# An mLSTM, a soft mixture of experts and a squared-ReLU MLP on one core: the output weights' remainders, two clears and the last copy are moved

## The chip, the cores and the metric

The kernel runs on one core of a Trainium2 chip. The metric is the device time of one execution in microseconds (us), lower is better. A core has five engines that run their own instruction streams in order and wait for each other by semaphores: TensorE (PE in the rows, its weight loads PEld), VectorE (DVE), ScalarE (ACT), GpSimd (POOL) and SyncE (SP). Here all DMAs are issued by SyncE. Matmuls write to PSUM, and everything else lies in SBUF.

## The reference

Three steps over 4 sequences of 768 tokens, 3072 tokens of width 320 in all. `logits`, `d` and `c` are those of a soft mixture: 32 slots gather weighted sums of tokens, 8 experts turn them into outputs, and each token takes a weighted sum of the slots.

```python
# 1. mLSTM with a stabilised exponential gate, 8 heads of 40: y
# 2. soft mixture of experts
logits = x @ phi                                   # x: 3072 x 320, phi: 320 x 32
d = exp(logits - logits.max(0)); d /= d.sum(0) + 1e-9
slot_input = (d.T @ x).reshape(E, 4, D)            # E = 8
for e in range(E):
    slot_out[e] = np.maximum(slot_input[e] @ w1[e], 0.0) @ w2[e]
c = exp(logits - logits.max(1)); c /= c.sum(1) + 1e-9
x = c @ slot_out.reshape(32, D)
# 3. MLP
r = np.maximum(x @ w_in, 0.0)                      # w_in: 320 x 2048
return (r * r) @ w_out                             # w_out: 2048 x 320
```

## The kernel before

**Stages.** From 0 to some 151 us of the profiled span the mLSTM runs chunk by chunk, with the mixture's first three sequences filled in between. From there to some 183 us (the passage, below) the last sequence's logits, the token sums, the experts and the preparation of the MLP follow each other. From 183 us to the end the MLP loop runs: 96 steps, 6 groups of 512 tokens (`tg`) by 16 blocks of 128 hidden features (`f`). Each step has one matmul for a later step's hidden block (L1472) and twelve for the output (L1546): four blocks of 128 tokens, three products each, since both factors are split into a rounded part and a remainder (`hi` and `los`, `wohl["h"]` and `wohl["l"]`).

**The order of the work is written out by hand** (a manual schedule): each engine runs its instructions in the order in which the code issues them. Generators are pieces of work advanced by `next` and run out by `finish`. `cgo(n)` advances the building of the table `cst[n]` of mixing weights (L1122 and L1124 on VectorE, transposes L1130 on TensorE, copy L1135 on ScalarE). The passage's own path is: token sums (L1229), `combine`, `ffn_up(0)` and `ffn_up(1)` (the experts' first matmuls, L1221, by halves of the hidden features), `relu` (L1276), `ffn_tr` (transposes, then the copy L1333 into the block-padded `hT`), `ffn_down(0)` to `ffn_down(7)` (L1350, all eight into one PSUM bank), the copy `sos` (L1402), its transposes (L1407) with the copies into `soT` (L1410), and `gp_mm` (L1428), the first matmul of the MLP.

**The output weights.** `w_out` comes as 16 blocks of 128 rows, and is rounded and split in pairs of blocks, 640 columns each; `f` names a pair by its first block. Each pair takes `narrow`: two ScalarE instructions (L144, L148) into two scratch tiles, and two of VectorE (L152, L156) that put them together; then `wo_put`: a ScalarE cast (L1385) gives the rounded part, and a VectorE subtraction (L1386) the remainder. Pairs 0, 2 lie in `wo0`, 4 in `x3`, 6 in `xTw`; pairs 8, 10 come into `stage` by one load, `load_wo(stage, 8, 4)`, and 12, 14 into `par` by another (L905, 128 x 2560 words, 1.31 MB each). `stage` holds expert weights that `ffn_down(0)` reads, so its load is issued behind that. Before the change pairs 0 to 6 are narrowed in the passage, all with the one scratch pair `par_t`, and put in it (6 excepted); pairs 8 to 14 are made in the MLP loop at the steps that `X8` and `WO` name.

**What else the change touches.** `xf` (an old token buffer, `x` in the rows) is cleared by VectorE for the slots' padded inputs ahead of the token sums (L1199); `hT` (in `ring`) is cleared by GpSimd (L1291); `repm`, a 0/1 matrix, is built by VectorE (L1279, L1284); `call_last` finishes the last mixing weights; the loop's output copies (L1555) are ScalarE's.

Of the kernel before, what the change touches and what calls it, by code (L numbers as in the profile page):

```python
# [8 lines left out]
F32 = mybir.dt.float32  # L9
# [19 lines left out]
AHEAD = 3  # L29
UP = ((2, 3), (4,))  # L30
MODE = "fffaaaaaaaaaaaaa"
W8 = 0
GM, GA = (0, 1, 4, 6), (1, 3)
W6, X8 = 3, (2, 4)
WO = (5, 7, 10)
LAST = {3: "PADNgGG", 2: "gGGA", 1: ""}
START = "~36 1f 1i 1m 1h 1p 1b 1aG 1B 1r 1u 1A 1v D0 2f 1l T0 T1 1q M0 2i E0 W0 K0 D0 M1 E1 ~6 2m D0 2p 2b 2aG K1 W2 P0 2h D0 2B 2r 2u P1 M2 2v E2 2A 2l K2 ~7 | 3f 3i D1 ~6 | D1 2q 3m 3h 3p | D1 3b 3aG 3B 3r | 3u D1 3A 3l 3v | D2 3q | D2 | D2 | D2 X |"
REBIAS = 2.0**-112
# [7 lines left out]
def kernel(  # L46
# [1149 lines left out]
        nc.vector.tensor_copy(craw(B1) if m else en[:, m].rearrange("p u s -> p (u s)"), t[:, 0:192])  # L1196

    nc.vector.tensor_reduce(out=se4[96:128], in_=t2[96:128, 0:B1], axis=AX.X, op=ALU.add)
    nc.vector.memset(xf[:, FF : FF + 80 * NE], 0.0)  # L1199
    tr_el(0)  # L1200
    finish(fd)
    warm(WD[4], dumt)
# [76 lines left out]
    nc.vector.tensor_scalar(  # L1279
        out=repm, in0=ident[:, 0:1].to_broadcast([128, 64 + 4 * 128]), scalar1=0.0, scalar2=None, op0=ALU.mult  # L1280
    )
    for n in range(4):
        for r in range(2):
# [8 lines left out]
    for n in range(6):
        ld_w2(ring_half(2 * (n % 3) + n // 3), *w2o[10 + n])
    cgo(1, 1)
    t = bank("m")
    nc.tensor.matmul(t[:, 0:1], lhsT=selJ.rearrange("p j i -> p (j i)"), rhs=rt[0:32], start=True, stop=True)
    nc.vector.tensor_copy(rt128, t[:, 0:1])
    relu(0)
    finish(wo_narrow(2, *par_t))
    tr_el(1)  # L1300
    lg = call[:, NC * (B1 - 1) : NC * B, :]
    cm = mp.tile([128, 12], F32, tag="cm", name="cm")
    nc.vector.tensor_reduce(out=cm, in_=lg, axis=AX.X, op=ALU.max)
    cc = el_.rearrange("p m t -> p (m t)")[:, 0:384].rearrange("p (n s) -> p n s", s=32)
    nc.vector.tensor_tensor(out=cc, in0=lg, in1=cm.unsqueeze(2).to_broadcast([128, 12, 32]), op=ALU.subtract)
# [87 lines left out]

    ffn_down(1)
    load_wo(par[1][:, 0:SLOT], 12, 4)
    wo_put(0)
    ffn_down(2)
    ffn_down(3)
    wo_put(2)
    for f in range(4, 8):  # L1400
        ffn_down(f)
    nc.scalar.copy(sos, so[:, 0:DM])  # L1402
    cgo(3, 3, 5)
    dumf = bank("o")
# [8 lines left out]
                .rearrange("p (j s) -> p j s", j=NP)[:, :, 0:8],  # L1413
            )
    cgo(4, 5, 4)
    wo_put(4)
    ws8 = wo_split(8)
    for _ in range(W8):
        next(ws8)
    gc = [slice(0, 128), slice(128, 512)]  # L1420
    gps = [bank("mb"), bank("m")]

# [91 lines left out]
        g_rep(n, gc[1], trep[:, 0:384])  # L1514
        (nc.scalar.copy if n in GA else nc.vector.tensor_copy)(gst[n + 1], trep[:, 0:384])

    def put6():
        yield
        wo_put(6)

    wos = {W6: [(put6(), 9)], X8[0]: [(ws8, 4 - W8)]}
    wos.setdefault(X8[1], []).append((ws8, 9))
    for k, b in enumerate(WO):
        wg = wo_split(10 + 2 * k)
        for d, n in ((0, 4), (1, 2), (2, 9)):
            wos.setdefault(b + d, []).append((wg, n))

    acc = None
    for i, (tg, f) in enumerate(steps):
        if len(UP) <= i < len(steps) - AHEAD:  # L1530
            up(*steps[i + AHEAD])
        for wg, n in wos.get(i, ()):
            for _ in range(n):
                next(wg, None)
        if f == 0:
            acc = [bbank("acc") for _ in range(4)]
        hi, lo = gh.pop((tg, f)), gl.pop((tg, f))
        ua = [(u, a) for u in range(4) for a in range(3)]
        if i == 0:
            ua.sort(key=lambda x: (x[0] // 2, x[1]))  # L1540
        for n, (u, a) in enumerate(ua):
            if i == 0 and n == 3:
                gp_mm(1, 2)
                gp_hl(1)
            l_, r_ = ((hi, "h"), (hi, "l"), (lo, "h"))[a]
            nc.tensor.matmul(  # L1546
                acc[u][:, 0:DM],
                lhsT=l_[:, 128 * u : 128 * u + 128],
                rhs=wohl[r_, f // 8][:, f % 8, :],
                start=(f == 0 and a == 0),  # L1550
                stop=(f == NF - 1 and a == 2),
            )
# [95 lines left out]
```

## Time and profile before

| | |
|---|---|
| median of 3 runs | 383.35 us (383.09 to 383.78) |
| the profiled execution | 383.42 us, of which the span from first to last instruction is 381.70 |
| granted TensorE clock | 1.00 |
| busy over the span | TensorE 373.2 us (98%), VectorE 265.1 (69%), ScalarE 257.8 (68%), GpSimd 102.3 (27%) |

Times in the rows are microseconds from the start of the span. TensorE's "busy" takes the modelled ends of its matmuls, so a busy stretch can hide a loss of some tenths; where it stood still it shows as an idle time in brackets behind a row, with the instruction that ended it. An engine's idle time matters only if TensorE, or the last DMA, waits for it.

### The profile page before, as it was taken

The page shows a single profiled execution, that of the slowest core. Times are in us where ns is not written, and L with a number is a line of the kernel's source. Part 1 is how long each engine was busy: PE and PEld are TensorE (multiplying, and loading weights), DVE is VectorE, ACT ScalarE, POOL GpSimd, SP SyncE. Part 2 cuts the span into 40 slices and gives each one's busy share as a digit, 9 for nine tenths or more (in the row PEclk, how much of TensorE's full clock was granted, in tenths as well). Part 3 has the DMA queues.
Part 4 walks back from the last instruction along what each step waited for, and adds up shares of the span by engine and source line. Part 5 has one row for each costly group of instructions (what it writes and reads, how often), then busy time and mean ns, then how long its engine had stood idle before and what let it go on. Part 6 is the DMA issues. An engine that isn't in the chain of part 4 may idle for free.

```text
span 381.7 us, 9179 instructions
## 1 busy us (share of the span) xinstructions
PE 373.2 (98%) x3435; PEld 333.0 (87%) x3435; DVE 265.1 (69%) x596; ACT 257.8 (68%) x592; POOL 102.3 (27%) x207
## 2 busy tenths in 40 slices
PE   8999999999999999999999999999999999999996
PEld 6889998889889886445799899999999999999996
DVE  7878888979898478667798955555555555555551
ACT  7798766668656855365797966576675667667662
POOL 5665976766677465200000000000000000000000
PEclk9999999999999999999999999999999999999999
DMA  6796897899959998895000020020020001002001
GB/s 180 229 345 209 286 318 221 261 328 341 327 172 374 316 388 300 290 371 244 3 0 0 2 69 3 0 70 1 2 69 2 1 2 69 3 0 70 0 3 69
DMA packets 19541, 56.62 MB, mean 148 GB/s; under 512 B 2481, under 2 KB 7561, under 8 KB 19113
## 3 DMA queue, kind: packets, MB, share of 16 engines
q1 hardware_dynamic: 19497, 56.04, 43.0%
q8 instruction: 27, 0.44, 0.5%
q14 instruction: 17, 0.14, 0.1%
HBM read 52.10 MB, written 3.93 MB: 147 GB/s over the span
## 4 chain that ended last, share of the span: by engine, by line
PE 86%; DVE 7%; POOL 2%; issue 2%; ACT 1%; POOLq 0%; DVEq 0%
PE ps_mb L1546 19%; PE ps_st L1546 17%; PE ps_lt L1546 9%; PE ps_st L475 8%; PE ps_o L575 5%; PE ps_o L1472 4%; PE ps_o L560 4%; PE ps_lt L201 2%; PE ps_st L1350 2%; PE ps_st L503 2%; PE ps_m L1472 2%; PE ps_mb L444 2%; DVE p L487 2%; PE ps_lt L726 2%; DVE x L657 2%
## 5 line engine op out<-in xcount | busy, mean ns | idle before, releaser
L1496 DVE CAST hi<-ring 128x512 fp32r<-128x512 f32 x93 | 39.7, 427 | 60.9 <-ACT ring L1495 52.7
L1497 DVE TENSOR_TENSOR los<-ring,hi 128x512 fp32r<-128x512 f32 x96 | 66.5, 692 | 9.8
L458 ACT ACTIVATE w<-ps_mb,qt 128x128 f32<-128x128 f32 x192 | 56.6, 368 | 15.5 <-PE ps_mb L444 10.2
L1477 ACT ACTIVATE ring<-ps_o 128x512 f32<-128x512 f32 x64 | 38.3, 598 | 34.1 <-PE ps_o L1472 34.1
L1495 ACT ACTIVATE ring<-ring 128x512 f32<-128x512 f32 x93 | 58.8, 632 | 2.9
L475 PE MATMUL ps_st<-par 120*128 120x128 f32 (+1 forms) x384 | 56.9, 284 | 0.0
L1546 PE MATMUL ps_mb<-wohlh,hi 128*128 128x320 f32 x160 | 49.4, 310 | 0.0
L1546 PE MATMUL ps_mb<-wohll,hi 128*128 128x320 f32 x160 | 49.3, 309 | 0.0
L1546 PE MATMUL ps_mb<-wohlh,los 128*128 128x320 f32 x160 | 49.2, 309 | 0.0
L475 PEld LDWEIGHTS ps_st<-par 120*128 120x128 f32 (+1 forms) x384 | 47.9, 191 | 0.2 <-DVE ring L399 0.2
L1546 PE MATMUL ps_st<-wohll,hi 128*128 128x320 f32 x144 | 44.6, 310 | 0.0
L1546 PE MATMUL ps_st<-wohlh,hi 128*128 128x320 f32 x144 | 44.5, 309 | 0.0
L1546 PE MATMUL ps_st<-wohlh,los 128*128 128x320 f32 x144 | 44.5, 309 | 0.0
L465 POOL TENSOR_SCALAR_AFFINE_SELECT w<-w 128x384 f32<-128x384 f32 (+1 forms) x66 | 37.3, 565 | 18.7 <-ACT w L458 13.4
L487 DVE TENSOR_TENSOR p<-ps_st,w 128x384 f32<-128x384 f32 (+1 forms) x66 | 35.5, 538 | 4.7 <-POOL w L465 3.6
L1477 ACT ACTIVATE ring<-ps_m 128x512 f32<-128x512 f32 x32 | 19.2, 599 | 18.3 <-PE ps_m L1472 18.3
L1546 PEld LDWEIGHTS ps_mb<-wohll,hi 128*128 128x128 f32 x160 | 29.9, 187 | 1.5
L1546 PEld LDWEIGHTS ps_mb<-wohlh,hi 128*128 128x128 f32 x160 | 30.0, 188 | 0.0
L1546 PEld LDWEIGHTS ps_mb<-wohlh,los 128*128 128x128 f32 x160 | 30.0, 188 | 0.0
L575 PE MATMUL ps_o<-par,p 128*64 128x41 f32 x768 | 29.0, 232 | 0.0
L1546 PEld LDWEIGHTS ps_st<-wohll,hi 128*128 128x128 f32 x144 | 27.0, 187 | 2.1 <-issue 0.6
L575 PEld LDWEIGHTS ps_o<-par,p 128*64 128x64 f32 x768 | 25.1, 137 | 3.9
(305 smaller groups left out, 777.4 us busy)
## 6 DMA issues: line engine op xcount, KB each, us to landing
ring<-in_w_dram SPq DMA_DIRECT2D x22, 640.0 KB
stage<-in_w_in_dram SPq DMA_DIRECT2D x10, 512.0 KB
par<-in_w_dram SPq DMA_DIRECT2D x6, 640.0 KB
out_dram<-ring SPq DMA_DIRECT2D x24, 160.0 KB
par<-in_v_s_dram SPq DMA_DIRECT2D x9, 369.0 KB
par<-in_k_s_dram SPq DMA_DIRECT2D x9, 360.0 KB
x<-in_o_gate_dram SPq DMA_DIRECT2D x9, 320.0 KB
par<-in_k_t_dram SPq DMA_DIRECT2D x23, 120.0 KB
```

The lines of the kernel that those rows point to most:

```text
L458: nc.scalar.activation(w[:, j, :], mb[:, 128 * j : 128 * j + 128], AF.Exp, bias=qt3[:, c, h0 + j : h0 + j + 1])
L465: nc.gpsimd.affine_select(out=w, in_=w, pattern=[[0, nh], [1, 128]], compare_op=ALU.is_ge, fill=0.0, base=0, channel_multiplier=-1)
L475: nc.tensor.matmul(st[:, 128 * j : 128 * j + 128], lhsT=kbd[g % 2][0:nd, j, ts_], rhs=qin[g][0:nd, ts_], start=True, stop=True,)
L487: nc.vector.tensor_tensor(out=p, in0=sts.pop((g, c))[:, 0 : nh * 128].rearrange("p (n t) -> p n t", n=nh), in1=ws.pop((g, c)), op=ALU.mult,)
L560: nc.tensor.matmul(pos[g, c // 2][:, o0 : o0 + nv], lhsT=qin[g][0:nd, 128 * c : 128 * c + 128], rhs=cbds[g, c - 1][0:nd], start=True, stop ...
L575: nc.tensor.matmul(po[t0 : t0 + 64, o0 : o0 + DV], lhsT=p[:, j, t0 : t0 + 64], rhs=vin[g][:, c, j, :], start=True, stop=True,)
L1472: nc.tensor.matmul(t, lhsT=gst[n][:, 128 * k : 128 * k + 128], rhs=cst[tg], start=True, stop=True)
L1477: nc.scalar.activation(r, t, AF.Relu)
L1495: nc.scalar.activation(r, r, AF.Square)
L1496: nc.vector.tensor_copy(hi, r)
L1497: eng.tensor_tensor(out=lo, in0=r, in1=hi.bitcast(F32), op=ALU.subtract)
L1546: nc.tensor.matmul(acc[u][:, 0:DM], lhsT=l_[:, 128 * u : 128 * u + 128], rhs=wohl[r_, f // 8][:, f % 8, :], start=(f == 0 and a == 0), sto ...
```

## The change

- The clear of `xf` on VectorE stands behind the token sums' scalar work (`tt`) and no longer ahead of `tr_el(0)`.
- `hT` is cleared by ScalarE (two copies of a broadcast column with scale 0), behind `relu(0)`, and no longer by GpSimd.
- `repm` is built later on VectorE.
- A second pair of scratch tiles, `par_u`, lies in free parts of `x3` and `xTw`. `begin_wo` issues the two ScalarE instructions of a pair; `finish` the two of VectorE. Pairs 0, 2, 4, 6 alternate between `par_t` and `par_u` and begin sooner.
- All four puts of pairs 0 to 6 stand ahead of `ffn_down(2)`; pairs 8 and 10 are narrowed ahead of the copy `sos`, and 8 is put ahead of `gp_mm`. In the loop 10 is put at step 2, 12 and 14 are made from steps 4 and 7.
- The last output copy is split: 160 columns on ScalarE, 160 on VectorE.

```diff
-W8 = 0
-W6, X8 = 3, (2, 4)
-WO = (5, 7, 10)
+W6 = 2
+WO = (4, 7)
...
-    nc.vector.memset(xf[:, FF : FF + 80 * NE], 0.0)
     tr_el(0)
...
     nc.vector.tensor_tensor(out=tt, in0=es, in1=se4, op=ALU.mult)
+    nc.vector.memset(xf[:, FF : FF + 80 * NE], 0.0)
...
+    x3f = x3.rearrange("p c d -> p (c d)")
     par_t = [par[i][:, PW - 690 : PW - 50] for i in range(2)]
+    par_u = [x3f[:, SLOT // 2 : SLOT // 2 + 2 * DM], xTw[:, SLOT // 2 : SLOT // 2 + 2 * DM]]
+
+    def begin_wo(f, ts):
+        g_ = wo_narrow(f, *ts)
+        next(g_)
+        next(g_)
+        return g_
...
+    g0 = begin_wo(0, par_t)
+    g2 = begin_wo(2, par_u)
     ffn_up(0, (2, 1, 3, 4))
...
-    cgo(2)
-    finish(wo_narrow(0, *par_t))
-    for h in range(2):
-        nc.gpsimd.memset(hT[:, 4 * h : 4 * h + 4], 0.0)
+    finish(g0)
+    g4 = begin_wo(4, par_t)
+    finish(g2)
+    cgo(2)
     for n in range(6):
         ld_w2(ring_half(2 * (n % 3) + n // 3), *w2o[10 + n])
     cgo(1, 1)
...
     relu(0)
-    finish(wo_narrow(2, *par_t))
+    for h in range(2):
+        nc.scalar.activation(
+            hT[:, 4 * h : 4 * h + 4].rearrange("p f (a w) -> p (f a) w", w=128),
+            ident.unsqueeze(1).to_broadcast([128, 8, 128]),
+            AF.Copy,
+            scale=0.0,
+        )
     tr_el(1)
+    g6 = begin_wo(6, par_u)
+    finish(g4)
...
+    finish(g6)
...
     ffn_up(1, range(3, 5))
+    cl = call_last()
+    next(cl)
     relu(1)
+    finish(cl)
...
-    n4, cl = wo_narrow(4, *par_t), call_last()
-    next(n4)
-    next(n4)
     ffn_down(0)
     ffn_tr(1)
-    next(cl)
-    finish(n4)
-    finish(cl)
-    finish(wo_narrow(6, *par_t))
     load_wo(stage, 8, 4)
...
-    cgo(3, 4)
...
     ffn_down(1)
     load_wo(par[1][:, 0:SLOT], 12, 4)
-    wo_put(0)
-    ffn_down(2)
-    ffn_down(3)
-    wo_put(2)
-    for f in range(4, 8):
+    for f in range(0, 8, 2):
+        wo_put(f)
+    for f in range(2, 8):
         ffn_down(f)
+    g8 = begin_wo(8, par_t)
+    g10 = begin_wo(10, par_u)
+    cgo(3, 4)
+    finish(g8)
+    finish(g10)
     nc.scalar.copy(sos, so[:, 0:DM])
     cgo(3, 3, 5)
...
     cgo(4, 5, 4)
-    wo_put(4)
-    ws8 = wo_split(8)
+    wo_put(8)
...
-    wos = {W6: [(put6(), 9)], X8[0]: [(ws8, 4 - W8)]}
-    wos.setdefault(X8[1], []).append((ws8, 9))
+    wos = {W6: [(put10(), 9)]}
     for k, b in enumerate(WO):
-        wg = wo_split(10 + 2 * k)
+        wg = wo_split(12 + 2 * k)
...
-                nc.scalar.copy(ot, acc[u][:, 0:DM])
+                cut = DM // 2 if i + 1 == len(steps) and u == 3 else DM
+                nc.scalar.copy(ot[:, 0:cut], acc[u][:, 0:cut])
+                if cut < DM:
+                    nc.vector.tensor_copy(ot[:, cut:DM], acc[u][:, cut:DM])
```

Three places in the engines' orders. Rows name line, operation, what is written and read, and its shape; line numbers are each kernel's own.

VectorE at the token sums, before (`en` is what the token sums' matmuls read, `rm`, `es`, `comb` and `tt` the scalar work beside them, `x` is `xf`):

```order
L1198 TENSOR_REDUCE se_120<-ps_o 32x1
L1199 MEMSET x 128x640
L1196 COPY en<-ps_mb 128x192
L1205 TENSOR_REDUCE rm<-ps_m 128x1
L1210 TENSOR_SCALAR comb<-selF,es 128x32
L1212 TENSOR_TENSOR tt<-es,se_120 128x1
```

and now:

```order
L1197 TENSOR_REDUCE se_120<-ps_o 32x1
L1195 COPY en<-ps_mb 128x192
L1203 TENSOR_REDUCE rm<-ps_m 128x1
L1208 TENSOR_SCALAR comb<-selF,es 128x32
L1210 TENSOR_TENSOR tt<-es,se_120 128x1
L1211 MEMSET x 128x640
```

The clear has moved from ahead of `en` to behind `tt`.

ScalarE from the second half's ReLU to the MLP's first matmul, before (`wohlh` is the rounded part, `ring<-ps_st 128x320` is the copy `sos`):

```order
L1276 ACTIVATE x<-ps_o,rt_2559 128x512
L144 ACTIVATE par_70<-x 128x640
L148 ACTIVATE par_71<-x 128x640
L1333 COPY ring<-ps_mb 128x32x4
L1308 ACTIVATE el<-el 128x384
L144 ACTIVATE par_70<-xTw 128x640
L148 ACTIVATE par_71<-xTw 128x640
L1385 CAST wohlh_2966<-wo_84 128x640 x2
L1402 COPY ring<-ps_st 128x320
L1135 CAST cst_3049<-ps_m 128x512
L1135 CAST cst_3072<-ps_o 128x512
L1385 CAST wohlh_2966<-x 128x640
```

and now:

```order
L1284 ACTIVATE x<-ps_o,rt_2559 128x512
L1352 COPY ring<-ps_mb 128x32x4
L1399 CAST wohlh_2966<-wo_84 128x640 x2
L1399 CAST wohlh_2966<-x 128x640
L1399 CAST wohlh_2966<-xTw 128x640
L143 ACTIVATE par_70<-stage 128x640
L147 ACTIVATE par_71<-stage 128x640
L143 ACTIVATE x<-stage 128x640
L147 ACTIVATE xTw<-stage 128x640
L1419 COPY ring<-ps_st 128x320
L1134 CAST cst_3061<-ps_m 128x512
L1134 CAST cst_3084<-ps_o 128x512
```

Four instructions that read `stage` now stand ahead of the copy `sos`; those of pairs 4 and 6 stand further up.

VectorE ahead of and behind the copies into `soT` (`ring<-ps_mb`; `chl` is the work for the tables `cst`, `wohll` a remainder, `gx` the first matmul's result), before:

```order
L1124 TENSOR_TENSOR chl<-call,chl 128x8x32
L1386 TENSOR_TENSOR wohll_2967<-wo_84,wohlh_2966 128x640 x2
L1122 CAST chl<-call 128x8x32
L1124 TENSOR_TENSOR chl<-call,chl 128x8x32
L1410 COPY ring<-ps_mb 128x32 x2
L1410 COPY ring<-ps_mb 64x32 x2
L1386 TENSOR_TENSOR wohll_2967<-x,wohlh_2966 128x640
L1439 TENSOR_TENSOR gx<-ps_mb,gx 128x128
```

and now:

```order
L1123 TENSOR_TENSOR chl<-call,chl 128x8x32
L151 SCALAR_TENSOR_TENSOR par_71<-stage,par_71 128x640
L155 SCALAR_TENSOR_TENSOR stage<-par_70,par_71 128x640
L151 SCALAR_TENSOR_TENSOR xTw<-stage,xTw 128x640
L155 SCALAR_TENSOR_TENSOR stage<-x,xTw 128x640
L1121 CAST chl<-call 128x8x32
L1123 TENSOR_TENSOR chl<-call,chl 128x8x32
L1427 COPY ring<-ps_mb 128x32 x2
L1427 COPY ring<-ps_mb 64x32 x2
L1400 TENSOR_TENSOR wohll_2969<-stage,wohlh_2968 128x640
L1453 TENSOR_TENSOR gx<-ps_mb,gx 128x128
```

Four VectorE instructions of pairs 8 and 10, and then the pair for `cst[5]`, now stand directly ahead of the copies into `soT`. TensorE's own order is the same before and after.

## Rows read from the trace of the kernel before

**Rows 1.** Stretches: us, busy us (instructions) by engine, PEclk, DMA share, GB/s

```profile
155.00:175.00 20.00, 20.00 (x216) 8.45 (x220) 15.09 (x38) 10.70 (x18) 1.92 (x2) 1.00 0.90 331
...
158.00:160.00 2.00, 2.00 (x24) 0.52 (x16) 1.94 (x8) 0.00 (x0) 1.14 (x2) 1.00 0.60 110
```

**Rows 2.** Waits of TensorE's matmuls from 145 us, the longest: total, times, longest

```profile
PE ps_lt L1546 <- DVE wohll L1386: 0.7, 1, 0.7
```

**Rows 3.** In order of time, token sums: start, us, instruction, [idle before <-releaser]

```profile
152.25 0.59 DVE L1199 MEMSET x<- 128x640 f32 x1 [0.20 <-issue]
152.87 0.36 DVE L1196 COPY en<-ps_mb 128x192 f32<-128x192 f32 x1
...
153.29 1.29 PE L1229 MATMUL ps_st<-x,en 128*32 128x128 f32 x24 [0.50 <-DVE en L1196]
```

**Rows 4.** Single lines: duration ns min/median/max, first and last start

```profile
L1284 DVE CAST repm<-ident x8: 161/511/914, 158.7 to 160.9; 32x32 fp32r<-32x32 f32 x8
...
L284 ACT ACTIVATE par<-ident x3: 1144/1144/1145, 2.2 to 4.3; 120x1152 f32<-120x1152 f32 x3
```

**Rows 5.** In order of time: the copy into `hT` and `ffn_down(0)`

```profile
165.54 0.26 ACT L1333 COPY ring<-ps_mb 128x128 f32<-128x128 f32 x1
...
167.02 1.26 PE L1350 MATMUL ps_st<-stage,ring 128*32 128x320 f32 x16
```

**Rows 6.** In order of time, SyncE: the last two weight loads' issue

```profile
168.34 0.33 SPq L905 DMA_DIRECT2D stage<-in_w_out_dram  x1
170.14 0.33 SPq L905 DMA_DIRECT2D par<-in_w_out_dram  x1
```

**Rows 7.** Stretches as in Rows 1; the last number is GB/s

```profile
171.00:174.50 3.50, 3.50 (x60) 1.69 (x56) 3.29 (x9) 2.91 (x4) 0.00 (x0) 1.00 0.91 347
174.50:177.00 2.50, 2.50 (x36) 1.17 (x28) 2.43 (x6) 0.39 (x1) 0.00 (x0) 1.00 0.98 414
177.00:178.00 1.00, 1.00 (x9) 0.75 (x7) 0.96 (x5) 0.62 (x2) 0.00 (x0) 1.00 0.54 219
178.00:180.00 2.00, 1.99 (x37) 1.11 (x36) 1.05 (x5) 1.48 (x3) 0.00 (x0) 1.00 0.06 20
```

**Rows 8.** In order of time, pair 6 on both engines

```profile
171.19 0.83 ACT L144 ACTIVATE par<-xTw 128x640 f32<-128x640 f32 x1 [1.26 <-issue]
...
171.93 0.82 ACT L148 ACTIVATE par<-xTw 128x640 int32<-128x640 uint16 x1
...
172.78 0.83 DVE L152 SCALAR_TENSOR_TENSOR par<-xTw,par 128x640 int32<-128x640 int32 x1
...
173.65 0.82 DVE L156 SCALAR_TENSOR_TENSOR xTw<-par,par 128x640 int32<-128x640 int32 x1
```

**Rows 9.** In order of time, the handover to the MLP

```profile
176.61 0.43 ACT L1402 COPY ring<-ps_st 128x320 f32<-128x320 f32 x1 [2.48 <-PE ps_st L1350]
...
177.18 0.29 DVE L1122 CAST chl<-call 128x256 fp32r<-128x256 f32 x1
...
177.47 1.23 PE L1130 MATMUL ps_o<-ident,chl 128*128 128x128 f32 x8
...
177.85 0.59 DVE L1410 COPY ring<-ps_mb 128x32 f32<-128x32 f32 x4
...
178.63 1.00 PE L1428 MATMUL ps_mb<-wi,ring 128*32 128x128 f32 x24
```

**Rows 10.** In order of time, the loop: one matmul L1472 a step

```profile
205.76 0.40 PE L1472 MATMUL ps_o<-cst,gst 128*128 128x512 f32 x1
...
214.39 0.81 DVE L1386 TENSOR_TENSOR wohll<-par,wohlh 128x640 fp32r<-128x640 f32 x1
...
216.98 0.40 PE L1472 MATMUL ps_o<-cst,gst 128*128 128x512 f32 x1
...
218.98 0.40 PE L1472 MATMUL ps_o<-cst,gst 128*128 128x512 f32 x1
```

**Rows 11.** In order of time, the last output copies

```profile
377.81 0.87 ACT L1555 COPY ring<-ps_mb 128x320 f32<-128x320 f32 x2
```

More of the change, by code (lines that the diff above doesn't have):

```diff
@@ L1276, in relu @@
         nc.scalar.activation(hsb[:, 512 * fh : 512 * fh + 512], hps[fh], AF.Relu, scale=rt128)
+    g0 = begin_wo(0, par_t)
+    g2 = begin_wo(2, par_u)
     ffn_up(0, (2, 1, 3, 4))
+    finish(g0)
+    g4 = begin_wo(4, par_t)
+    finish(g2)
+    cgo(2)
+    for n in range(6):
+        ld_w2(ring_half(2 * (n % 3) + n // 3), *w2o[10 + n])
+    cgo(1, 1)
+    t = bank("m")
+    nc.tensor.matmul(t[:, 0:1], lhsT=selJ.rearrange("p j i -> p (j i)"), rhs=rt[0:32], start=True, stop=True)
+    nc.vector.tensor_copy(rt128, t[:, 0:1])
+    relu(0)
+    for h in range(2):
[5 more added lines that the diff above has]
+        )
+    tr_el(1)
+    g6 = begin_wo(6, par_u)
+    finish(g4)
+    lg = call[:, NC * (B1 - 1) : NC * B, :]
+    cm = mp.tile([128, 12], F32, tag="cm", name="cm")
+    nc.vector.tensor_reduce(out=cm, in_=lg, axis=AX.X, op=ALU.max)
+    cc = el_.rearrange("p m t -> p (m t)")[:, 0:384].rearrange("p (n s) -> p n s", s=32)
+    nc.vector.tensor_tensor(out=cc, in0=lg, in1=cm.unsqueeze(2).to_broadcast([128, 12, 32]), op=ALU.subtract)
     nc.vector.tensor_scalar(
@@ L1287 @@
             )
-    cgo(2)
-    finish(wo_narrow(0, *par_t))
-    for h in range(2):
-        nc.gpsimd.memset(hT[:, 4 * h : 4 * h + 4], 0.0)
[L1292 to L1298, printed above, removed]
-    finish(wo_narrow(2, *par_t))
[L1300 to L1305, printed above, removed]
+    finish(g6)
     def call_last():
@@ L1415 @@
     cgo(4, 5, 4)
-    wo_put(4)
-    ws8 = wo_split(8)
-    for _ in range(W8):
-        next(ws8)
+    wo_put(8)
     gc = [slice(0, 128), slice(128, 512)]
@@ L1515, in more, with put10 @@
         (nc.scalar.copy if n in GA else nc.vector.tensor_copy)(gst[n + 1], trep[:, 0:384])
-    def put6():
+    def put10():
         yield
-        wo_put(6)
-    wos = {W6: [(put6(), 9)], X8[0]: [(ws8, 4 - W8)]}
-    wos.setdefault(X8[1], []).append((ws8, 9))
+        wo_put(10)
+    wos = {W6: [(put10(), 9)]}
     for k, b in enumerate(WO):
-        wg = wo_split(10 + 2 * k)
+        wg = wo_split(12 + 2 * k)
         for d, n in ((0, 4), (1, 2), (2, 9)):
```

## The prediction

> **What bounds the kernel now.** First the stretches of the span, then TensorE's waits, then the instructions in order of time around each wait. From 155 to 175 us TensorE is busy for 20.00 of 20 us, VectorE for 15.09, ScalarE for 10.70, and the granted clock is 1.00 [rows 1]. So in the passage the other engines cost nothing unless TensorE runs into them. It does so at two places that this change can reach. Ahead of the token sums TensorE stands still for 0.50 us until VectorE has copied `en`, which came behind the clear of `xf` [rows 3]. In the loop it waits for the remainder of pair 14 [rows 2]: VectorE has it at 214.39 + 0.81 = 215.20, and the five steps from 205.76 to 216.98 take 11.22 us where a step takes 2.00 (216.98 to 218.98), so 1.2 us are lost, the wait's 0.7 and what the modelled ends hide [rows 2, 10]. All else that TensorE does is work, and its order stays. So the most that the change can win is 0.5 + 1.2 and a little at the end. What it can lose is decided at the handover to the MLP, where nothing can be done for TensorE until `sos` and `soT` are copied.
>
> **The change part by part.**
>
> *Clear of `xf`.* 0.59 us go from ahead of `en` [rows 3]. The copy then starts when its transposes are through, some 0.4 us sooner, and TensorE's work down to `ffn_down(7)` shifts by as much: -0.4, if nothing later waits for something that doesn't shift. Behind `tt` the clear lies beside the token sums' 1.29 us of matmuls; without that cover it would cost 0.59 again.
>
> *GpSimd's clear of `hT`, and `repm`.* `repm`'s eight small copies take 161 to 914 ns, and start from 158.7 to 160.9, while GpSimd clears [rows 4]; at 161 each they would take 1.3 us, some 1.1 less. That is VectorE's time, beside TensorE's work: 0 on the path.
>
> *`hT` on ScalarE.* The trace's row for such a clear has 1144 ns for 1152 columns [rows 4]; 1024 columns are 1.02 us by proportion, two are 2.0. They stand between `relu(0)` and the copy into `hT`, with two narrowing instructions as before. `relu(0)` comes sooner: VectorE no longer does `repm` ahead of `rt128` (some 2.8 us with the clear ahead of its copies) but pair 2 (1.65, see below), and gains the 0.4. So the copy comes at 165.54 - 1.2 - 0.4 + 2.0 = 165.9, and `ffn_down(0)` wants it at 167.02 - 0.4 = 166.6 [rows 5]: nothing lost, with 0.7 to spare. If that cover is gone, each tenth moves `ffn_down(0)`, and what is issued behind it.
>
> *Pairs 0 to 6 sooner.* The same instructions in other gaps. ScalarE's two for pair 4 wait for their load and for VectorE's pair 0, and `cst[1]` and `relu(0)` are queued behind them. Traffic falls to 110 GB/s in 158 to 160, against 331 over the whole stretch [rows 1]: the queue ran dry, so that load had landed when ScalarE gets there, near 159.5. The earlier puts of 4 and 6 add two casts and two subtractions in the passage; they end by some 175, when both engines wait anyhow (next): 0.
>
> *Pairs 8 and 10 ahead of `sos`: the term that decides.* ScalarE runs in order. It now has four instructions that read `stage` ahead of the copy `sos`, and VectorE four of the same pairs, then the work for `cst[5]`, ahead of `soT`. `stage` is loaded behind `ffn_down(0)`: issued at 168.34, and the next load at 170.14 [rows 6], 1.31 MB each, 2.62 together. From 171 on 3.5 x 0.347 + 2.5 x 0.414 + 0.219 + 2 x 0.020 = 2.51 MB flow [rows 7], so these two loads are nearly all of that traffic, one behind the other, and the first 1.31 MB are through at 174.5. A reader needs the last of the 16 DMA engines, and they end unevenly: the traffic falls over 177 to 180 and doesn't stop at once [rows 7]. With 1.9 us for that the load is in at 176.4; issued 0.4 sooner, at **L = 176.0**. Before, pair 8 was first read in the loop, so nobody waited for it.
>
> From L, with pair 6's rows as the price [rows 8]: ScalarE's instructions follow at 0.74 (171.19 to 171.93), the fourth ends at 3 x 0.74 + 0.82 = L + 3.0, and `sos` is copied then. VectorE starts pair 8 at 0.74 + 0.82 = L + 1.6; a pair takes 0.87 + 0.82, say 1.65, so pair 10 ends at L + 4.9. The work for `cst[5]` is 0.67 (177.18 to 177.85) [rows 9]: L + 5.5. Its four transposes on TensorE stand ahead of `gp_mm`, half of 1.23 [rows 9]: **`gp_mm` starts at L + 6.1**, while `soT` is copied beside them. That is 182.1 against 178.63 [rows 9]: **+3.5**. The 0.4 of the clear is in it already, as the earlier issue. On TensorE the only cover in these us are transposes, some 2 us, that it had before too.
>
> The bounds of this term are those of L. If all DMA engines ended together, L = 174.5 - 0.4 = 174.1, and the term is 1.6. If they trail for as long as the traffic does at the end, to 180 [rows 7], L is near 177.5, and the term is 5.0. I take 176.0, since the traffic has fallen from 414 to 219 GB/s in 177 to 178 and is nearly gone in 178 to 180.
>
> A rule speaks against this term. The Trainium skill, "DMA: Bandwidth & Descriptors", section "Anatomy of one DMA", gives a DMA some 2.0 us plus its bytes by 436 GB/s; as an estimate from that page 1.31 MB issued at 168.34 would be in at 173.3, which is the first rival's case. Here the load stands in a queue behind others, and the traffic rows bear out the later time. The same page ("Why a DMA increments its semaphore by 16 and not by 1") says that only the count of all engines means landed, which is why the last one is what I ask for.
>
> *The loop.* Pairs 8 and 10 are narrowed ahead of it, 12 and 14 are put at steps 6 and 9, and 14 is read at step 14: the late remainder is some five steps early. -1.2 [rows 10]. If the stall has another cause it stays: 0.
>
> *The last copy.* Two copies took 0.87 [rows 11]; half of one on each engine saves at most 0.2, I take -0.1.
>
> **The sum.** The profiled execution took 383.42 us, 381.70 of them span; the median of the runs is 383.35, 0.07 below, which I neglect. 383.42 + 3.5 - 1.2 - 0.1 = 385.6. With the term's bounds: 383.42 + 1.6 - 1.3 = 383.7, and 383.42 + 5.0 - 1.3 = 387.1.
>
> **The rivals.**
>
> *Faster: `stage` is there when ScalarE comes for it.* Then the order costs only what it adds to VectorE ahead of `soT`: two pairs and two subtractions, 3.3 + 1.6 = 4.9 us, against 20 - 15.09 = 4.9 us of idle time there [rows 1] and 1.1 that `repm` gets back, less what of the idle time lies at the wrong place. Between all of it hidden (-0.4 - 1.2 - 0.1: 381.7) and 0.9 on the path (382.6) I say 382.2. It decides at `gp_mm`: L would have to lie below 178.6 - 6.1 = 172.5 for no loss there, or below 173.8 for no loss in all. For it: the load is issued 8 us ahead of `sos`. Against it: 1.31 MB can't flow by then at the rows' rates. The skill's fit above gives L = 173.3 and some 382.9.
>
> *Slower still: TensorE's clock falls in the new wait.* It would have little to do between 176.1 and 182.1. At the lower of the two levels each us of its work takes two, from `gp_mm` until the clock is back; for one to four us of such work that is 386.6 to 389.6, I say 388. No row here shows a clock below 1.00, and the transposes break the gap. The Trainium skill, "TensorE: Matmul & The Clock Gate", section "What's actually happening", says that an idle TensorE falls to half its clock and that activity gives it back.
>
> *The loop's stall stays* because it was the engines' backlog and not pair 14's place: 385.6 + 1.2 = 386.8.
>
> **How the numbers follow.** Forecast 0.70, with its own range from 383.7 to 387.1; `stage` in time 0.12; clock 0.10; stall stays 0.08. Faster or slower means by over 0.2%, 0.77 us, about what a measurement of this kernel can tell from no change: below 382.6 or above 384.1. Most of the first rival is faster, 0.11. Within lie the rest of it and the low end of the forecast's L (below 174.6): 0.10. Slower: 0.79. The range from 383.7 to 387.4 leaves out the first rival and the upper part of the clock's case, 0.19 together.
>
> **What would show it.** Right: ScalarE idle up to some 176 ahead of the first instruction that reads `stage`, ended by that load; `sos` copied near 179, `soT` near 181.5; TensorE waiting some 3 us ahead of `gp_mm`, in two pieces about the transposes; no wait for a remainder in the loop, and all steps near 2.00 us; token sums 0.4 sooner. Wrong: `sos` copied near 176.2 with pair 8 narrowed ahead of it (then L is wrong), a clock below 1.00 from 178 on, or `ffn_down(0)` later than 166.7 (then `hT`'s clear wasn't covered).

## The result: slower, by more than was forecast

| | before | after |
|---|---|---|
| median of the runs, us | 383.32 (383.09 to 383.78, 6 runs) | 388.10 (386.78 to 389.54, 6 runs) |
| profiled execution, us | 383.42 | 387.24 |
| its span, us | 381.70 | 385.50 |
| mean granted clock | 1.000 (profiled one) | 0.987 to 0.996 (6 runs) |

The ratio is 1.0123, with an interval of 1.0094 to 1.0152. The forecast was 385.6 us in a range of 383.7 to 387.4: the direction was right, the median lies 0.7 above the range. The six runs of the changed kernel stand in three groups by their mean clock: 0.996 (386.78, 387.01), 0.991 (387.24, the profiled one) and 0.987 (388.96, 388.96, 389.54).

**The profile after.** First TensorE's waits from 145 us on (total, times, longest). The row of before [rows 2], the loop's wait for `wohll`, is gone, and the one ahead of the token sums [rows 3] isn't among them either. Two new ones stand ahead of `gp_mm`:

```profile
PE ps_mb L1424 <- ACT ring L1419: 2.0, 1, 2.0
PE ps_o L1129 <- DVE ring L1427: 0.8, 1, 0.8
```

L1419 is the copy `sos`, L1427 the copies `soT`. Around them, in order of time, first ScalarE, then VectorE, then TensorE (start, us, instruction, and in brackets the idle time before it and what ended it):

```profile
175.47 0.81 ACT L143 ACTIVATE par<-stage 128x640 f32<-128x640 f32 x1 [3.31 <-DMA stage<-in_w_out_dram]
...
177.55 0.76 ACT L147 ACTIVATE xTw<-stage 128x640 int32<-128x640 uint16 x1
178.22 0.40 ACT L1419 COPY ring<-ps_st 128x320 f32<-128x320 f32 x1
...
176.98 0.83 DVE L151 SCALAR_TENSOR_TENSOR par<-stage,par 128x640 int32<-128x640 int32 x1 [2.31 <-ACT par L147]
...
179.58 0.82 DVE L155 SCALAR_TENSOR_TENSOR stage<-x,xTw 128x640 int32<-128x640 int32 x1
...
180.98 0.59 DVE L1427 COPY ring<-ps_mb 128x32 f32<-128x32 f32 x4
...
178.68 0.90 PE L1424 MATMUL ps_mb<-ident,ring 128*128 128x128 f32 x3 [2.04 <-ACT ring L1419]
...
181.21 1.09 PE L1129 MATMUL ps_o<-ident,chl 128*128 128x128 f32 x4 [0.78 <-DVE ring L1427]
182.23 1.66 PE L1442 MATMUL ps_mb<-wi,ring 128*32 128x128 f32 x24
```

This answers to [rows 9]. ScalarE has nothing to do for 3.31 us, until `stage` has landed; then its four instructions of pairs 8 and 10 run, and only then `sos`: at 178.22, where it was 176.61. VectorE follows with the same pairs, and `soT` comes at 180.98 where it was 177.85. `gp_mm` starts at 182.23 for 178.63, and its 24 matmuls take 1.66 us for 1.00.

That last number is the clock. The stretches of the trace (us, busy us and instructions by engine, granted clock, DMA share, GB/s):

```profile
175.00:180.00 5.00, 2.96 (x26) 1.97 (x19) 2.81 (x4) 3.62 (x6) 0.00 (x0) 0.87 0.39 157
180.00:185.00 5.00, 4.22 (x39) 1.74 (x37) 2.62 (x9) 1.48 (x3) 0.00 (x0) 0.50 0.00 0
185.00:190.00 5.00, 4.86 (x36) 2.61 (x33) 2.94 (x5) 3.50 (x7) 0.00 (x0) 0.95 0.01 2
```

From 180 to 185 us TensorE runs at 0.50, the lower of its two levels (1.2 GHz of 2.4). The 0.87 and 0.95 beside it are the fall and the return, near 178.7 and 185.5 (finer stretches stand in the last section); elsewhere in the passage and the loop it is at 1.00. In before all three stretches have 1.00. So the loop begins 5.03 us later, not 3.6. The first of its matmuls, before and after:

```profile
183.08 0.41 PE L1546 MATMUL ps_lt<-wohlh,hi 128*128 128x320 f32 x1
```

```profile
188.11 0.41 PE L1559 MATMUL ps_lt<-wohlh,hi 128*128 128x320 f32 x1
```

The first of the last output copies, before and after:

```profile
376.93 0.43 ACT L1555 COPY ring<-ps_lt 128x320 f32<-128x320 f32 x1 [4.46 <-PE ps_lt L1546]
```

```profile
380.74 0.43 ACT L1569 COPY ring<-ps_lt 128x320 f32<-128x320 f32 x1 [4.46 <-PE ps_lt L1559]
```

It comes 3.81 later, so the loop gave 1.2 us back: from its first matmul to this copy it takes 192.63 us for 193.85. The account of the profiled execution: 3.1 (the handover, at full clock, from the second experiment) + 1.9 (the clock) - 1.2 (the loop) = 3.8; 387.24 - 383.42 = 3.8.

### The profile page after: what moved, and what is told of

Its sections match the earlier page's. It is cut to its first block, busy times and chain, and to the rows that moved or that the text cites. A ratio compares the mean times of both kernels' runs of the same rounds, so it can differ in the third digit from the quotient of the medians.

```text
span 385.5 us, 9184 instructions
## 1 busy us (share of the span) xinstructions
PE 374.1 (97%) x3435; PEld 333.6 (87%) x3435; DVE 264.0 (68%) x597; ACT 259.6 (67%) x594; POOL 100.4 (26%) x205
## 4 chain that ended last, share of the span: by engine, by line
PE 84%; DVE 6%; DMA 3%; ACT 2%; POOL 2%; issue 2%; SPq 0%; DVEq 0%; POOLq 0%
PE ps_mb L1559 18%; PE ps_st L1559 17%; PE ps_lt L1559 9%; PE ps_st L474 9%; PE ps_o L574 5%; PE ps_o L559 4%; PE ps_o L1486 4%; PE ps_st L502 2%; PE ps_mb L443 2%; DMA stage<-in_w_out_dram 2%; PE ps_m L1486 2%; PE ps_lt L725 2%; PE ps_m L716 1%; DVE p L486 1%; PE ps_st L1220 1%
```

## The experiments

Every kernel was timed beside the kernel before on the same chip, whose medians there were 383.27, 383.42, 383.64 and 383.65 us.

### Pairs 8 and 10 back in the loop

The theory: all of the loss comes from narrowing pairs 8 and 10 ahead of `sos`. The rival: some other part of the change (ScalarE's clear, the earlier pairs 0 to 6) costs as well. Against the changed kernel:

```
-    g8 = begin_wo(8, par_t)
-    g10 = begin_wo(10, par_u)
     cgo(3, 4)
-    finish(g8)
-    finish(g10)
     nc.scalar.copy(sos, so[:, 0:DM])
...
-    wo_put(8)
+    ws8 = wo_split(8)
...
-WO = (4, 7)
+X8 = (2, 4)
+WO = (5, 7, 9)
```

> The changed kernel with pairs 8 and 10 made in the loop again (pair 8 in steps 2 and 4, pair 10 from 5, 12 from 7, 14 from 9), all else as changed. If the wait for the stage load ahead of sos is the whole loss: 381.8 us (381.4 to 382.5), granted clock 1.00, gp_mm near 178.2. If another edit costs (hT on ScalarE, pairs 0 to 6 sooner): above 383.3.

Measured: 382.58 us (381.87 to 383.22, 7 runs), ratio 0.9982 (0.9970 to 0.9993). ScalarE's row of `sos`, and TensorE's only wait after 145 us:

```profile
175.80 0.43 ACT L1415 COPY ring<-ps_st 128x320 f32<-128x320 f32 x1 [3.91 <-PE ps_st L1372]
```

```profile
PE ps_lt L1552 <- DVE los L1507: 0.2, 1, 0.2
```

`sos` waits for TensorE again, not for a load. With all other parts of the change in place the kernel is faster than before, by 0.7 us, so the two pairs carry the whole loss: 388.1 - 382.6 = 5.5 us. The time is 0.8 us above the expected 381.8 and just outside its range; which of the small terms fell short, the single parts below tell.

### The clock held by unused matmuls

The changed kernel with matmuls on zeros in its two waits:

```
     cgo(3, 3, 5)
+    warm(16)
     dumf = bank("o")
...
-    cgo(4, 5, 4)
+    cgo(4)
+    warm(6)
+    cgo(5, 4)
```

> The changed kernel with 16 extra small matmuls ahead of sos's transposes and 6 ahead of the last table's, which only keep TensorE busy. If the clock's fall is what came on top of the forecast: clock 1.00, gp_mm near 181.6, 385.1 us (384.6 to 385.7) in all runs alike. If the clock costs nothing and the wait alone is longer than forecast: 387 to 389 as the changed kernel.

Measured: 385.88 us (385.36 to 386.19, 4 runs), ratio 1.0067 (1.0052 to 1.0082). The instructions on ScalarE stand where they stood (`stage` read at 175.47, `sos` at 178.22). The stretches, and `gp_mm`:

```profile
175.00:180.00 5.00, 4.57 (x48) 3.40 (x41) 2.81 (x4) 3.94 (x7) 0.00 (x0) 1.00 0.42 171
180.00:185.00 5.00, 4.11 (x52) 2.39 (x54) 3.00 (x10) 2.03 (x6) 0.00 (x0) 1.00 0.00 0
```

```profile
181.21 0.63 PE L1129 MATMUL ps_o<-ident,chl 128*128 128x128 f32 x4 [0.89 <-DVE ring L1428]
181.77 1.00 PE L1445 MATMUL ps_mb<-wi,ring 128*32 128x128 f32 x24
```

The handover is as late, the clock is at 1.00, the transposes take 0.63 us again for 1.09 and `gp_mm` 1.00 for 1.66. The loop starts at 186.2, 1.9 us sooner than in the changed kernel, and the median lies 0.2 above the range expected for a held clock. So the medians split the loss: the clock is 388.1 - 385.9 = 2.2 us, and the handover with all other terms 385.88 - 383.27 = 2.6 us, close to the forecast's 2.25.

### The load in two halves, and the load second

If the landing of `stage` sets the handover, then half a load that pair 8 can start on brings everything forward, and a load issued behind the other moves everything back. Against the changed kernel, first one, then the other:

```
-    load_wo(stage, 8, 4)
+    load_wo(stage[:, 0 : SLOT // 2], 8, 2)
+    load_wo(stage[:, SLOT // 2 : SLOT], 10, 2)
```

```
-    load_wo(stage, 8, 4)
...
     load_wo(par[1][:, 0:SLOT], 12, 4)
+    load_wo(stage, 8, 4)
```

> The changed kernel with the stage load in two halves, pair 8 ahead of pair 10, 0.66 MB each. If the load's landing sets the handover: pair 8 begins near 173.7, pair 10 near 175.5, sos near 177.0, gp_mm near 180.0, waits under 1 us each, clock 1.00 or nearly: 383.4 us (383.0 to 384.8). If the backlog of VectorE and ScalarE sets it and not the load: gp_mm at 181.5 or later and 387 as the changed kernel.

> The changed kernel with the stage load issued behind the load for pairs 12 and 14, so that it lands some 3 us later, near 178.5. If the landing sets the handover: gp_mm later by as much, 185 or more, and the clock down for longer: 390.5 us (389.5 to 393.5). If the backlog sets it: 387 to 389.

Measured: 384.05 us with two halves (383.49 to 385.64, 10 runs), ratio 1.0026 (1.0013 to 1.0039); 391.44 us with the load second (390.73 to 393.76, 4 runs), ratio 1.0224 (1.0190 to 1.0259). ScalarE's first instruction on `stage`, in the one and in the other:

```profile
174.08 0.83 ACT L143 ACTIVATE par<-stage 128x640 f32<-128x640 f32 x1 [1.88 <-DMA stage<-in_w_out_dram]
```

```profile
180.11 0.77 ACT L143 ACTIVATE par<-stage 128x640 f32<-128x640 f32 x1 [7.15 <-DMA stage<-in_w_out_dram]
```

`sos` follows at 176.97 and at 182.79: 2.9 and 2.7 us behind the landing, as in the changed kernel (2.75). `gp_mm` starts at 180.45 and 186.82. The second landing is 1.6 us later than was expected, and the time lies in the range given all the same. TensorE's wait ahead of the transposes is 0.77 us with two halves, and the one ahead of `gp_mm` 1.47, longer than the 1 us expected. The profiled execution's clock is 1.00 throughout, but one run of the ten has a mean of 0.996, and it is the slowest (385.64; the other nine take 383.49 to 384.85). With the load second the first wait is 5.86 us, and the clock is gone for longer (the profiled execution is the slowest of the four):

```profile
180.00:185.00 5.00, 1.74 (x7) 1.32 (x7) 3.21 (x5) 3.58 (x6) 0.00 (x0) 0.65 0.00 0
185.00:190.00 5.00, 4.21 (x38) 1.86 (x37) 2.21 (x8) 1.48 (x3) 0.00 (x0) 0.50 0.00 0
190.00:195.00 5.00, 5.00 (x21) 3.15 (x21) 1.94 (x3) 2.43 (x5) 0.00 (x0) 0.50 0.00 2
```

So the landing sets the handover: 1.4 us sooner or 4.6 later, it takes `sos` along by 1.2 and 4.6. The clock's loss comes on top.

### Single parts on the kernel before

First the clear of `xf` alone, then the last split one step sooner alone:

```
-    nc.vector.memset(xf[:, FF : FF + 80 * NE], 0.0)
...
     nc.vector.tensor_tensor(out=tt, in0=es, in1=se4, op=ALU.mult)
+    nc.vector.memset(xf[:, FF : FF + 80 * NE], 0.0)
```

```
-WO = (5, 7, 10)
+WO = (5, 7, 9)
```

> The kernel before, with one part of the change alone: the clear of the padded x (161 ns on VectorE) is issued behind the token sums instead of ahead of them. Prediction's term: the token sums start 0.4 us sooner and all behind them too, 383.3 - 0.4 = 382.9 us; by the trace of the changed kernel (token sums at 152.79 for 153.29) 0.5, so 382.8. Rival, that a later wait (the loads of output weights, or the loop's stall on the remainder of pairs 10 and 11) swallows it: 383.3. The run with the pairs 8 and 10 put back into the loop came 0.8 us short of the sum of the small terms, so one of these terms must be smaller than it was priced.

> The kernel before, with the last split of output weights (pair 14 and 15) begun one step of the loop sooner (step 9 for step 10), nothing else. It tells whether the loop's wait for the remainders can be had by order alone, and what it is worth: the trace of before shows the loop's matmuls waiting for wohll. If that wait goes and nothing takes its place: 383.3 - 1.1 = 382.2 us. If the wait is for an earlier pair, or work in the loop that is now moved delays something else by as much: 383.3.

Measured: the clear (0.59 us in [rows 3]; the 161 ns in the expectation is a slip) 383.09 us (382.66 to 383.32, 11 runs), ratio 0.9988 (0.9979 to 0.9997), so 0.5 us by the ratio, with 0.1 to 0.8 as its interval; the split 383.65 us (383.05 to 383.81, 11 runs), ratio 1.0002 (0.9993 to 1.0011), nothing. The split's trace tells why. The wait for `wohll` is gone, and two others stand in the loop in its place:

```profile
PE ps_lt L1546 <- DVE los L1497: 0.2, 1, 0.2
PE ps_lt L1546 <- DVE hi L1496: 0.2, 1, 0.2
```

VectorE now makes the remainder sooner and the parts `hi` and `los` of the loop's own activations later: moved by one step and nothing else, the remainder delays its neighbours. The loop's matmuls of one kind, from first to last start, here and in the first experiment (193.2 us from 183.1 to 376.3 in before, 192.0 from 188.1 to 380.1 in the changed kernel):

```profile
L1546 PE MATMUL ps_lt<-wohlh,hi x80: 307/310/417, 183.4 to 376.6; 128*128 128x320 f32 x80
```

```profile
L1552 PE MATMUL ps_lt<-wohlh,hi x80: 307/310/414, 182.3 to 374.8; 128*128 128x320 f32 x80
```

The split leaves the loop at 193.2 us. The first experiment has the same pairs at the same steps, but pair 6 is put ahead of its loop, and it takes 192.5: 0.7 less. So work taken off VectorE and ScalarE in the loop shortens it, where the order alone did not. That answers the gap of the first experiment: in the traces its loop gave 0.7 us for the forecast's 1.2 and the clear 0.4 (below), 1.1 together, where its median moved 0.7 with an interval of 0.3 to 1.1.

### A wait alone, in three lengths

Is the wait enough to bring the clock down, without the change? In the kernel before, extra copies of the sums' bank into a free tile stand ahead of `sos` (4, 6 and 10 of them; the result doesn't use them):

```
+    for _ in range(4):
+        nc.scalar.copy(x3.rearrange("p c d -> p (c d)")[:, SLOT // 2 : SLOT // 2 + DM], so[:, 0:DM])
     nc.scalar.copy(sos, so[:, 0:DM])
```

> The kernel before, with four extra copies of the sums' bank (426 ns each by the trace of before, 1.7 us in all) on ScalarE just ahead of the copy sos, and no other edit: the changed kernel's handover delay (sos 178.22 for 176.61) without any of its pairs. Theory A, the wait alone brings TensorE's clock down, as in the changed kernel: 383.3 + 1.7 + about 2 = 387, with a granted clock under 1.00 between 175 and 190 us. Theory B, the clock holds at a wait of this size (the changed kernel had a second wait of 0.78 us behind its first of 2.04): 383.3 + 1.7 = 385.0, granted clock 1.00.

> The kernel before with six extra copies (2.55 us) on ScalarE ahead of sos, between the four that left the clock at 1.00 (TensorE's wait 1.7 us, 385.2 us) and the ten that did not (4.4 us, 389.8 us). TensorE's wait here should be 2.6 us, the sum of the changed kernel's two waits (2.04 and 0.78) in one piece. If the clock falls: some 383.4 + 2.7 + 1 to 2 = 387 to 388 us, granted clock under 1.00 in some stretch between 175 and 190 us. If it holds: 383.4 + 2.7 = 386.1 us, and the changed kernel's fall would need another reason than the length of its waits.

> As the short one, with ten extra copies (4.2 us) ahead of sos. If only the wait's length counts: 383.3 + 4.2 = 387.5 us. If the clock follows the wait, as where the stage load went second (a wait of 5.86 us, granted clock 0.50 to 0.65, 391.4 us): half clock for some 5 us behind the wait, 2 to 4 us on top, 389.5 to 391.5. If the short one holds the clock and this one does not, the clock's fall has a point between the two waits; if both lose it, then each further us of wait costs about 1 us and the clock's part is nearly the same in both.

Measured: 385.20 us (384.95 to 385.44, 4 runs) with four copies, 386.00 (385.98 to 386.26, 4 runs) with six, 389.84 (388.81 to 390.56, 4 runs) with ten; ratios 1.0045, 1.0064 and 1.0164. TensorE's new wait in the three, in that order:

```profile
PE ps_mb L1409 <- ACT ring L1404: 1.7, 1, 1.7
```

```profile
PE ps_mb L1409 <- ACT ring L1404: 2.6, 1, 2.6
```

```profile
PE ps_mb L1409 <- ACT ring L1404: 4.4, 1, 4.4
```

The clock is 1.00 in all stretches of the first two, and no run of theirs has a mean below 0.998. The stretches with six copies:

```profile
175.00:180.00 5.00, 2.43 (x32) 1.26 (x24) 2.72 (x6) 3.36 (x8) 0.00 (x0) 1.00 0.47 195
180.00:185.00 5.00, 5.00 (x60) 2.85 (x57) 2.29 (x8) 2.98 (x8) 0.00 (x0) 1.00 0.00 0
```

With ten copies it falls, in all four runs (means of 0.991 to 0.995):

```profile
180.00:185.00 5.00, 3.22 (x31) 2.48 (x35) 1.21 (x5) 3.33 (x8) 0.00 (x0) 0.73 0.00 0
```

With four and six copies the kernel loses about the wait (1.8 us for 1.7, 2.4 for 2.6); with ten it loses 6.4 us for 4.4. So a wait by itself, with none of the change, brings the clock down, and the loss is then more than the wait. But its length doesn't decide alone: 2.6 us in one piece left the clock up in four runs of four, and the changed kernel's 2.04 and 0.78 us brought it down in six of six. Why, stays open.

### A little cover

Six unused matmuls in the first wait only, in the changed kernel:

```
     cgo(3, 3, 5)
+    warm(6)
     dumf = bank("o")
```

> The changed kernel with six unused matmuls on zeros ahead of the transposes (sixteen of them, with six more ahead of the second wait, held the clock and gave 385.9 us): TensorE's first wait is cut from 2.04 us to about 1.4 and begins some 0.6 us later, the second of 0.78 us is left as it is. It tells how much cover the clock needs, since one wait of 2.6 us ahead of sos in the kernel before left the clock at 1.00 (386.0 us) and the changed kernel's 2.04 did not. If the clock holds: 385.9 us, as with both waits filled. If it falls as in the changed kernel: 388.1 us. Runs of both kinds in one kernel would say that a wait of this size lies at the edge.

Measured: 386.91 us (385.22 to 387.75, 6 runs), ratio 1.0076 (1.0055 to 1.0096). The waits of the profiled execution, and the stretch in which its clock fell:

```profile
PE ps_o L1129 <- DVE ring L1428: 1.6, 1, 1.6
PE ps_mb L1425 <- ACT ring L1419: 1.4, 1, 1.4
```

```profile
182.00:184.00 2.00, 2.00 (x27) 0.89 (x25) 0.62 (x1) 0.00 (x0) 0.00 (x0) 0.50 0.00 0
```

Neither of the two expected times fits all runs: two have a mean clock of 1.000 and take 385.22 and 385.45 us, four have 0.996 and take 386.88 to 387.75. In the profiled execution the clock fell in the second wait. The first wait did shrink, to 1.4 us, but the second grew from 0.78 to 1.6: `soT` doesn't come sooner, and the transposes between are through sooner at the higher clock. So one program can hold the clock in one run and lose it in the next, and the two kinds of runs give the price of a fall here, about 1.4 to 2.5 us.

### `hT` cleared by GpSimd again, and a version with pair 8 alone

Both start from the kernel with the pairs back in the loop. The first only gives the clear to GpSimd. The second makes pair 8 ahead of `sos` from the first half of a load in two, and leaves pair 10 to the loop:

```
-        nc.scalar.activation(
-            hT[:, 4 * h : 4 * h + 4].rearrange("p f (a w) -> p (f a) w", w=128),
-            ident.unsqueeze(1).to_broadcast([128, 8, 128]),
-            AF.Copy,
-            scale=0.0,
-        )
+        nc.gpsimd.memset(hT[:, 4 * h : 4 * h + 4], 0.0)
```

```
+    g8 = begin_wo(8, par_t)
     cgo(3, 4)
+    finish(g8)
     nc.scalar.copy(sos, so[:, 0:DM])
...
-X8 = (2, 4)
-WO = (5, 7, 9)
+X8 = 2
+WO = (4, 6, 8)
```

> The run with pairs 8 and 10 in the loop, and with the clear of hT given back to GpSimd at the same place in the program: it tells whether moving that clear to ScalarE moves the end at all. The prediction put it at nothing on the path. If so: the same as that run, 382.6 us (0.998 of before). Rival, that the copies of repm on VectorE (2.43 us each beside GpSimd's clear in the trace of before, 1.08 us without it) hold back the products behind them: 382.6 + 1 = 383.6 us or more, and TensorE waits for VectorE between 160 and 172 us.

> A version that might beat both kernels: the stage load in two halves, pair 8 alone made ahead of sos (its half was there at 174.08 us in the run with the load in two), pair 10 back in the loop, with the remainders of pairs 10, 12 and 14 one or two steps sooner. If sos is not held up (ScalarE done with pair 8 at 175.6, before sos at 175.8) and the loop loses its waits for remainders (194.1 us from first to last start in the run with both pairs in it, 193.6 with none): 382.6 - 0.5 = 382.1 us. If the narrowing of pair 8 on ScalarE or VectorE delays sos or the copies soT: 382.6 to 384. Pair 8 alone ahead then costs what it gives.

Measured: 382.56 us (382.12 to 382.71, 6 runs) with GpSimd's clear, ratio 0.9970 (0.9958 to 0.9982); 382.42 (381.81 to 383.24, 9 runs) with pair 8 alone, ratio 0.9970 (0.9960 to 0.9980). GpSimd's clear costs nothing on the path, and ScalarE's gains nothing: the two intervals overlap. But the first doesn't test the rival it named (whose 2.43 and 1.08 us are those of all eight copies together), since in this order the clear is over before `repm` is made (its two parts start at 158.7 and 159.6, the copies from 165.3 on):

```profile
L1315 DVE CAST repm<-ident x8: 163/171/178, 165.3 to 166.2; 32x32 fp32r<-32x32 f32 x8
```

In the second, pair 8's half is there in time and no wait of TensorE is listed after 145 us any more. ScalarE's first instruction on it, and the loop:

```profile
173.24 0.85 ACT L143 ACTIVATE par<-stage 128x640 f32<-128x640 f32 x1 [1.03 <-DMA stage<-in_w_out_dram]
```

```profile
L1557 PE MATMUL ps_lt<-wohlh,hi x80: 307/310/417, 182.6 to 374.6; 128*128 128x320 f32 x80
```

With pair 10 narrowed in the loop and pair 8 ahead of it, the loop takes 192.0 us, as in the changed kernel. Whether the missing pair or the places one or two steps sooner did it isn't separated.

Both beat the two kernels, by 1.1 to 1.2 us against before. Which of the three versions without the late handover is the best, these runs can't tell.

## Why the prediction was wrong, point by point

**The step that failed is the clock.** The prediction forecast the new wait, in two pieces about the transposes, and then priced the fall of TensorE's clock in it as a separate case with a chance of 0.10, for two reasons: that no row showed a clock below 1.00, and that the transposes break the gap. Neither was a reason to leave it out. The rows of before had no wait of that size (the longest from 145 us on is 0.7, in the loop [rows 2]), so they could show no fall; and the transposes between the waits didn't prevent one. In these waits it fell in every run of the changed kernel. It is a term that the sum needed, +1.9 us in the profiled execution and 2.2 between the medians, and it varies from run to run with the time for which the clock stays down. Its price, 388 us when taken as a case (2.4 above the forecast), was close. The working behind it had two us for each us of TensorE's work; `gp_mm` took 1.66 us at 0.50 for 1.00, and the last transposes 1.09 for 0.63.

The Trainium skill, "TensorE: Matmul & The Clock Gate", section "What's actually happening", says that an idle TensorE drops to half its clock, and that the number of slow matmuls at a kernel's start changes from run to run. The trace agrees with the first (0.50 from 180 to 185 us), and for a gap in a kernel's middle the runs show the like of the second: one kernel has runs at 1.000 and at 0.996.

**The load's landing** was forecast for 176.0, and ScalarE starts on it at 175.47. Its issue:

```profile
167.90 0.33 SPq L904 DMA_DIRECT2D stage<-in_w_out_dram  x1
```

That is 0.44 sooner than [rows 6] (forecast: 0.4), and 7.6 us from the issue to the reader for 1.31 MB, with the DMA engines busy for 0.97 of the stretch from 170 to 175 us. The Trainium skill's fit ("DMA: Bandwidth & Descriptors", "Anatomy of one DMA"), as an estimate from that page, would have had it in at 172.9. The page measured its fit on DMAs that GpSimd issues, and the prediction used it for one that SyncE issues behind others; for such a load the measurement decides against it.

**From the landing on** the chain was right: `sos` 2.75 us behind it (forecast 3.0), `gp_mm` 6.3 behind it where the clock was held (forecast 6.1). At full clock the term is 181.77 - 178.63 = +3.1 for the forecast's +3.5, and with the clock held the kernel takes 385.9 for the forecast's 385.6. The first rival, `stage` in time, is out: ScalarE waited 3.31 us for it.

**Pairs 0 to 6 sooner**: forecast nothing. ScalarE starts pair 4 at 159.46 (forecast: near 159.5), released by VectorE and not by the load, and no wait of TensorE comes of these pairs.

**The clear of `xf`**: forecast -0.4. The copy of `en` and the token sums, as in [rows 3]:

```profile
152.37 0.36 DVE L1195 COPY en<-ps_mb 128x192 f32<-128x192 f32 x1 [0.42 <-PE ps_mb L1194]
```

```profile
152.79 1.29 PE L1228 MATMUL ps_st<-x,en 128*32 128x128 f32 x24
```

The sums start 0.50 sooner. Of this 0.11 was there ahead of the moved clear already (VectorE's reduction of `se` starts at 151.78 for 151.89), so 0.4 is the clear's, as forecast; the part alone measured 0.5 (0.1 to 0.8).

**`hT` on ScalarE**: forecast 2.0 us for two clears, the copy at 165.9, `ffn_down(0)` at 166.6. ScalarE, then TensorE, to be read with [rows 5]:

```profile
162.32 2.00 ACT L1301 ACTIVATE ring<-ident 128x1024 f32<-128x1024 f32 x2
...
165.61 0.25 ACT L1352 COPY ring<-ps_mb 128x128 f32<-128x128 f32 x1
...
166.52 1.26 PE L1372 MATMUL ps_st<-stage,ring 128*32 128x320 f32 x16
```

It takes 2.00, the copy comes at 165.61, and `ffn_down(0)` starts at 166.52. Nothing was lost there, as forecast, and by the GpSimd experiment nothing was won either.

**`repm`**: its eight copies take 163 to 178 ns each, at 165.0 to 165.9, for 161 to 914 [rows 4]. That is VectorE's time, and was rightly put at nothing on the path.

**The loop**: forecast -1.2, measured -1.2 in the trace of after, with the steps at 2.00 us where before lost its time [rows 10]:

```profile
204.79 0.39 PE L1486 MATMUL ps_o<-cst,gst 128*128 128x512 f32 x1
206.79 0.40 PE L1486 MATMUL ps_m<-cst,gst 128*128 128x512 f32 x1
```

The third rival, that the stall stays, is out. The reason was only half right: pair 14's remainder one step sooner, alone, gave nothing (three steps, as in the changed kernel, weren't tried alone), and pair 6's put out of the loop gave 0.7. So VectorE's and ScalarE's work in the loop counts, as that rival had it; how the rest is shared between less work and earlier places isn't separated.

**The last copy**: forecast -0.1, nothing was gained. VectorE's half doesn't run beside ScalarE's but behind it:

```profile
381.62 0.73 ACT L1569 COPY ring<-ps_mb 128x320 f32<-128x320 f32 x2
...
382.38 0.32 DVE L1571 COPY ring<-ps_mb 128x160 f32<-128x160 f32 x1 [4.85 <-ACT ring L1569]
```

The last of it ends 1.96 us behind the first copy's start, for 1.75 in before [rows 11]; from that start to the end of the span it is 4.8 us in both. It wasn't tried alone.

## What to carry to other kernels

When a step that reads a load is moved ahead of a copy that TensorE waits for, work out when the last piece of that load lands, from the issue and the bytes that are ahead of it in the queue; in the sum the copy comes behind that. If this makes TensorE stand still where it was busy (here for 2.04 and 0.78 us), a fall of its clock belongs into the sum, as a term with a range (here 0.9 to 3.7 us, the runs' 386.8 to 389.5 against 385.9 with the clock held), even if no row of the old kernel shows one. A remainder that comes late in a loop can be a sign that the engine that makes it has too much to do there: here moving it alone only delayed its neighbours, and taking work away helped.

## What was not expected of the hardware

The clock's fall doesn't follow the length of the wait. In the changed kernel it stood at 1.00 all through the first wait, which began at 176.64, and fell as the transposes began:

```profile
178.00:178.50 0.50, 0.00 (x0) 0.00 (x0) 0.50 (x1) 0.50 (x2) 0.00 (x0) 1.00 0.05 20
178.50:179.00 0.50, 0.33 (x2) 0.33 (x3) 0.50 (x2) 0.50 (x2) 0.00 (x0) 0.69 0.05 20
...
185.50:186.00 0.50, 0.50 (x6) 0.50 (x6) 0.00 (x0) 0.16 (x1) 0.00 (x0) 0.99 0.00 0
```

With ten extra copies it fell some 4.9 us after its wait had begun (at 177.38), when TensorE was at work again:

```profile
182.00:182.50 0.50, 0.50 (x6) 0.50 (x5) 0.14 (x2) 0.21 (x1) 0.00 (x0) 0.81 0.00 0
```

A wait of 2.6 us in the kernel before passed without a fall in four runs, while with the load in two halves (waits of 0.77 and 1.47 us in the profiled execution) one run of ten shows one by its mean clock. Once down, it stayed down through work without a gap: `gp_mm` from 182.23 on ran at 0.50 until 185.5. So here the wait is paid for behind itself, by whatever TensorE does next, and one trace isn't enough to price it: the same program took from 386.78 to 389.54 us.
